# The last four heads' gate logits carried as eight more value columns through the attention

## The chip, the cores and the metric

The program runs on one core of a Trainium2 chip. Its time is the device time of one execution in microseconds; the median of three runs before the change is 687.24 us (686.25 to 689.11). Five instruction streams matter: PE (TensorE, with PEld for its weight loads), DVE (VectorE), ACT (ScalarE), POOL (GpSimd) and SP, which here only issues DMAs, one after the other.

## The reference

Four batches of eight heads, 768 positions, head dimension 64. Attention is masked: a query sees the keys whose six sign bits (of a product with `proj`) equal its own. The attention output is laid out as x, 3072 tokens by 512 (eight heads side by side), and goes into a mixture of eight experts in which every token gets one expert, greedily by its logit and with 384 tokens an expert.

```python
mask = q_bucket[:, :, :, None] == k_bucket[:, :, None, :]
scores = np.where(mask, scale * np.matmul(q, k.transpose(0, 1, 3, 2)), -1e9)
attn = np.exp(scores - np.max(scores, axis=-1, keepdims=True))
attn = attn / (np.sum(attn, axis=-1, keepdims=True) + 1e-09)
x = np.matmul(attn, v).transpose(0, 2, 1, 3).reshape(B * S, H * D)
logits = x @ w_gate                    # 3072 x 8
for idx in np.argsort(-logits.flatten()):
    tok, e = idx // E, idx % E         # first free place of the best logit
    if assigned[tok] >= 0 or counts[e] >= cap: continue
    assigned[tok] = e; counts[e] += 1
out[assigned == e] = np.maximum(x[assigned == e] @ w1[e], 0.0) @ w2[e]
```

The order of the logits decides, so they are kept near float32 by pairs of f16 or bf16 parts (a high part and the remainder).

## The kernel before, in words

The 32 heads are worked in eight groups G of four (two groups a batch; a group's tiles alternate between two buffers, u = G%2). Work advances in steps t, six to a head, and each step has two half slots 2t and 2t+1; `add(n, f, ...)` hangs a function on half slot n, and the numbers in the table `AP` say which. The instructions of each engine run in the order in which this loop writes them; there is no other scheduler.

For a head, in steps: `S_pass` (L240) computes a score tile for the row maxima, which DVE takes (L242, m), and `m_rows` (L248, L249) writes them into rows 96 to 127 of QA; these passes run about nine steps ahead. `ST` (L258, L259) computes the scores again, transposed and with the maximum taken off, into a `psT` bank (three of them), and ACT takes the exponential (L260, pt). `lo` (L263) makes the low part of pt, on POOL or, where the table `XL` names the step, on DVE. `AV` (L273 to L275), four steps later, multiplies by the values: 18 matmuls a step, of 65 or 64 columns (64 value columns and one of ones, which gives the row sum) into the only `psV` bank; after a head's sixth step six matmuls with WF (L279, L280) take off the masked keys' share. `norm` (L287 to L290) divides and writes x; after every second head the two are stored to `x_dram`. `xtr` (L300 to L302) transposes two heads' x with PE into XH and XL, and `logits` (L309 to L311) multiplies by the gate weights `wgs`.

The values reach VH (f16) by `cv` on ACT and VL (remainder) by `sv` on POOL. `sumv` and `sumw` (L204 to L214) sum them into WF.

On SP: `load` fetches q, k and v of the next group (768 KB each), `moves` copies the casts into QA, KA, QB, KB and the sign rows bt into rows 64 to 69, and `clear` (L191) writes zeros into rows 96 to 127 of the QA buffer that the next group uses, 192 KB. A score pass reads all 128 rows of QA, so it needs its group's clear, casts and signs.

After head 31 the routing starts: `best` (L496 to L520) and then phase 0 of `Moe.phase`, a long chain of short DVE and PE steps that ends in the row numbers of the first expert's tokens; those are gathered from `x_dram` (xg, L762), the weights wf are fetched (L770), and the two layers of eight experts follow on PE.

Of the kernel before, what the change touches and what calls it, by code (L numbers as in the profile page):

```python
# [45 lines left out]
def attention(tc, nc, ctx, qT, kT, vv, proj, wg, x_dram, L, jp, identf, B, late=None, after=None):  # L46
# [9 lines left out]
    LD={}  # L56
# [27 lines left out]
    wgs=cp.tile([128,4,2,8],F16,name="wgs")  # L84
# [107 lines left out]
    def cv(G,j): A.copy(VH[G%2][:,j,:,0:64],LD[G][2][:,j])  # L192
    def sv(G,j,e=None): (e or V).tensor_tensor(VL[G%2][:,j],LD[G][2][:,j],VH[G%2][:,j,:,0:64],op=ALU.subtract)
    SQ={}
    def sumv(G):
        u=G%2
        if G<2:
            A.copy(WF[u][96:128,:,64],wc[96:128,:].to_broadcast([32,4]))
        ps=psT.tile([128,512],F32,name="pst")
        n=0  # L200
        for c in range(6):
            for src in (VH[u],VL[u]):
                g=32*(n%4)
                T.matmul(ps[g:g+32,0:256].rearrange("p (j d) -> p j d",j=4),on,src[:,:,c,0:64],start=n<4,stop=n>7,skip_group_check=True,tile_position=(0,g)); n+=1  # L204
        SQ[G]=dp.tile([128,256],F32,name="sq",bufs=1)
        A.copy(SQ[G],ps[:,0:256])
    def sumw(G):
        u=G%2
        ps=psT.tile([128,512],F32,name="pst")
        T.matmul(ps[:,0:256],onf,SQ[G],start=True,stop=True)  # L210
        pv=ps[96:128,0:256].rearrange("p (j d) -> p j d",j=4)
        hi=dp.tile([128,4,64],F16,name="shi",bufs=1)
        A.copy(hi[96:128],pv)
        V.scalar_tensor_tensor(WF[u][96:128,:,0:64],hi[96:128],ml[96:128],pv,op0=ALU.mult,op1=ALU.add)  # L214
# [49 lines left out]
    AVt={}  # L264
    def AV(h,kc):
        G,j=divmod(h,4); u=G%2
        if kc==0: AVt[h]=psV.tile([128,512],F32,name="psv")
        av=AVt[h][:,0:390].rearrange("p (c d) -> p c d",c=6)
        p,l=PT[h,kc]
        ph=p.bitcast(BF)[:,1::2]  # L270
        for c in range(6):
            r=slice(c*128,c*128+128)
            T.matmul(av[:,c,:],ph[:,r],VH[u][:,j,kc,:],start=(kc==0 and c==0),stop=False,skip_group_check=True)  # L273
            T.matmul(av[:,c,0:64],ph[:,r],VL[u][:,j,kc,:],start=False,stop=False,skip_group_check=True)  # L274
            T.matmul(av[:,c,:],l[:,r],VH[u][:,j,kc,:],start=False,stop=False,skip_group_check=True)  # L275
        if kc==5:
            for c in range(6):

                if j==3: T.matmul(av[:,c,:],QA[u][96:128,j,c*128:c*128+128],WF[u][96:128,j,:],start=False,stop=(c==5),skip_group_check=True,tile_position=(96,0))  # L279
                else: T.matmul(av[:,c,:],QA[u][:,j,c*128:c*128+128],WF[u][:,j,:],start=False,stop=(c==5),skip_group_check=True)  # L280
    X={}
    def norm(h):
        b,hh=divmod(h,8)
        if hh==0: X[b]=dp.tile([128,6,512],F32,name="X")
        av=AVt[h][:,0:390].rearrange("p (c d) -> p c d",c=6)
        r=dp.tile([128,6],F32,name="r6")
        V.tensor_scalar(r,av[:,:,64],1e-9,None,op0=ALU.add)  # L287
# [9 lines left out]
    def xtr(b,d,hf):  # L297
# [17 lines left out]
    def add(n,f,*a): at.setdefault(n,[]).append((f,a))
# [16 lines left out]
    def slots(G): return AP['P1'] if G==1 else AP['P2'] if G==2 else AP['P3'] if G==3 else [48*(G-1)+x for x in AP['P4']]  # L332
# [15 lines left out]

    k=12; done={}; half={}; S_at={}
# [589 lines left out]


@with_exitstack
def tile_bucket_attention_moe(ctx, tc, qT, kT, vv, proj, wg, w1, w2, out):
    nc = tc.nc
    B = qT.shape[0] // 2
    drp = ctx.enter_context(tc.tile_pool(name="drp", bufs=1, space=DR))
    x_dram = drp.tile([768 * B, 512], F32, name="x_dram")
    M = Moe(tc, nc, ctx, 768 * B)
    late = M.consts()
    with ExitStack() as c1:
        c1.enter_context(tc.manual_schedule())  # L950
        attention(tc, nc, c1, qT, kT, vv, proj, wg, x_dram, M.Lm, M.jp, M.identf, B, late, M.early)
# [39 lines left out]
```

## Time and profile before

| what | value |
|---|---|
| median of three runs | 687.24 us |
| the profiled execution | 686.77 us |
| its span, first to last instruction | 685.0 us |
| outside the span | 1.8 us |
| busy share of the span | PE 97%, POOL 76%, DVE 73%, ACT 69% |
| chain that ended last, by engine | PE 78%, DVE 8%, DMA 6%, ACT 3% |

The attention fills the first 372 us, the routing's phase 0 the next 25, the experts the rest. In the attention every engine is busy most of the time, so a stretch has to be read by itself. A busy PE is read with care: a matmul's duration overlaps the next one's, so its price is the distance from one start to the next.

### The profile page before, as it was taken

How to read it: one execution, taken by the hardware profiler on the slowest of the kernel's cores; microseconds unless marked ns; L12 is line 12 of the kernel's file. 1: busy time of each engine (PE TensorE's matmuls, PEld its weight loads, DVE VectorE, ACT ScalarE, POOL GpSimd, SP SyncE). 2: the span in 40 equal slices, each digit the busy share in tenths (PEclk: the TensorE clock that was granted, in tenths of full speed). 3: DMA queues.
4: the chain of work that ended last, by engine and by line, in shares of the span. 5: the costliest groups of instructions: out<-in, count | busy, mean ns of one | idle time of the engine just before them, and what ended most of it. 6: DMA issues, size and time to landing. Idle time of an engine off the chain costs nothing.

```text
span 685.0 us, 19366 instructions
## 1 busy us (share of the span) xinstructions
PE 661.1 (97%) x7952; PEld 435.0 (64%) x7952; DVE 499.7 (73%) x1124; ACT 471.4 (69%) x887; POOL 518.8 (76%) x456
## 2 busy tenths in 40 slices
PE   8899999999999999999998799999999999999997
PEld 3567676777777777777766575555555555655553
DVE  6778889888877887878884688778777887734120
ACT  7879887888878878877764054765665656666760
POOL 7999997997998989988655156586776665779871
PEclk9999999999999999999999599999999999999999
DMA  8646755526546266340000161717271726271701
GB/s 228 196 117 209 176 167 137 136 82 164 166 110 164 72 150 175 93 105 25 25 24 28 57 237 27 282 47 292 62 277 55 284 83 242 77 277 67 272 32 46
DMA packets 40241, 93.59 MB, mean 137 GB/s; under 512 B 4581, under 2 KB 30553, under 8 KB 37849
## 3 DMA queue, kind: packets, MB, share of 16 engines
q1 hardware_dynamic: 33048, 46.21, 25.3%
q0 software_dynamic: 7104, 46.15, 19.0%
q8 instruction: 62, 1.02, 0.6%
q14 instruction: 27, 0.21, 0.1%
HBM read 59.53 MB, written 12.58 MB: 105 GB/s over the span
## 4 chain that ended last, share of the span: by engine, by line
PE 78%; DVE 8%; DMA 6%; ACT 3%; issue 2%; POOL 1%; SPq 1%; POOLq 0%; DVEq 0%; ACTq 0%
PE po L870 14%; PE px L858 13%; PE pst L258 9%; PE pst L259 8%; PE pss L240 8%; PE psv L273 5%; PE psv L275 5%; PE psv L274 4%; PE pst L300 2%; DMA wf<-in_w_dram,zwidx 2%; DVE m L242 1%; PE po L858 1%; PE pst L248 1%; DVE lo L263 1%; PE pss L142 1%
## 5 line engine op out<-in xcount | busy, mean ns | idle before, releaser
L263 POOL TENSOR_TENSOR lo<-pt 128x768 f16<-128x768 f32 x144 | 226.3, 1585 | 35.9 <-ACT pt L260 33.0
L260 ACT ACTIVATE pt<-pst 128x384 f32<-128x384 f32 x384 | 181.8, 491 | 59.0 <-PE pst L259 49.3
L242 DVE TENSOR_REDUCE m<-pss 128x1 f16<-128x770 f32 x192 | 181.2, 956 | 34.0 <-PE pss L240 32.7
L258 PE MATMUL pst<-qa,ka 128*128 128x384 f16 x384 | 125.1, 326 | 3.8 <-ACT qa L249 2.8
L259 PE MATMUL pst<-qb,kb 128*128 128x384 f16 x384 | 124.8, 325 | 0.0
L273 PE MATMUL psv<-vh,pt 128*128 128x65 f16 x1152 | 120.7, 194 | 0.5 <-DVE X L290 0.5
L275 PE MATMUL psv<-vh,lo 128*128 128x65 f16 x1152 | 120.8, 194 | 0.0
L274 PE MATMUL psv<-vl,pt 128*128 128x64 f16 x1152 | 120.8, 193 | 0.0
L273 PEld LDWEIGHTS <-pt 128*128 128x128 bf16 x1152 | 106.7, 98 | 8.7 <-issue 0.6
L274 PEld LDWEIGHTS <-pt 128*128 128x128 bf16 x1152 | 105.6, 99 | 8.8 <-issue 0.7
L275 PEld LDWEIGHTS <-lo 128*128 128x128 f16 x1152 | 105.8, 97 | 0.0
L797 POOL TENSOR_TENSOR wl<-wf,wh 128x512 f16<-128x512 f32 x74 | 83.7, 1157 | 21.5 <-ACT wf L788 20.9
L240 PE MATMUL pss<-ka,qa 128*128 128x385 f16 x384 | 94.0, 328 | 1.5 <-DMA ka<-bt 0.7
L779 ACT ACTIVATE wh<-wf 128x1024 f16<-128x1024 f32 x64 | 66.9, 1054 | 31.7 <-DMA wf<-in_w_dram,zwidx 31.7
L858 PEld LDWEIGHTS <-wh 128*128 128x128 f16 x480 | 45.3, 97 | 29.8 <-issue 0.8
L263 DVE TENSOR_TENSOR lo<-pt 128x768 f16<-128x768 f32 x48 | 61.1, 1273 | 1.9 <-ACT pt L260 1.8
L870 PEld LDWEIGHTS <-hh 128*128 128x128 f16 x384 | 35.8, 97 | 38.4 <-issue 0.4
L788 ACT ACTIVATE wf<-wf 128x1024 f32<-128x1024 f32 x55 | 57.9, 1059 | 0.9
L240 PEld LDWEIGHTS <-qa 128*128 128x128 f16 x384 | 37.0, 97 | 27.1 <-DMA qa<-bt 1.4
L875 ACT ACTIVATE o<-po 128x512 f32<-128x512 f32 x23 | 13.7, 597 | 56.8 <-PE po L870 51.4
L259 PEld LDWEIGHTS <-kb 128*128 128x128 f16 x384 | 37.4, 97 | 18.8 <-issue 6.8
L770 POOL DMA_INDIRECT wf<-in_w_dram,zwidx x22 | 25.6, 1163 | 30.6 <-DVE zSTb L661 12.0
(296 smaller groups left out, 1359.7 us busy)
## 6 DMA issues: line engine op xcount, KB each, us to landing
vp<-in_vv_dram SPq DMA_DIRECT2D x8, 768.0 KB
x_dram<-X SPq DMA_DIRECT2D x16, 384.0 KB
qp<-in_qT_dram SPq DMA_DIRECT2D x7, 768.0 KB
kp<-in_kT_dram SPq DMA_DIRECT2D x7, 768.0 KB
qa<-qh SPq DMA_DIRECT2D x14, 192.0 KB
qb<-qh SPq DMA_DIRECT2D x14, 192.0 KB
ka<-kh SPq DMA_DIRECT2D x14, 192.0 KB
kb<-kh SPq DMA_DIRECT2D x14, 192.0 KB
```

What stands on the lines that cost most here:

```text
L240: T.matmul(ps[:,hf,0:HK],QA[u][:,j,qc*128:qc*128+128],KA[u][:,j,hf*HK:hf*HK+HK],start=True,stop=True)
L242: V.tensor_reduce(M6[h][:,qc:qc+1],ps[:,:,0:HK],axis=AX.XY,op=ALU.max,negate=True)
L258: T.matmul(ps[:,0:384],KA[u][:,j,kr],QA[u][:,j,r],start=True,stop=False)
L259: T.matmul(ps[:,0:384],KB[u][:,j,kr],QB[u][:,j,r],start=False,stop=True)
L260: A.activation(PT[h,kc][0][:,r],ps[:,0:384],AF.Exp,scale=0.125)
L263: eng.tensor_tensor(l,p,p.bitcast(BF)[:,1::2],op=ALU.subtract)
L273: T.matmul(av[:,c,:],ph[:,r],VH[u][:,j,kc,:],start=(kc==0 and c==0),stop=False,skip_group_check=True)
L274: T.matmul(av[:,c,0:64],ph[:,r],VL[u][:,j,kc,:],start=False,stop=False,skip_group_check=True)
L275: T.matmul(av[:,c,:],l[:,r],VH[u][:,j,kc,:],start=False,stop=False,skip_group_check=True)
L797: for _ in range(n): s.nc.gpsimd.tensor_tensor(*s.pend.pop(0)[1],op=ALU.subtract)
L858: T.matmul(p[:,0:384],a[:,o:o+128],b[:,d],start=n==0,stop=n==11)
L870: T.matmul(p,a[:,f,c*128:c*128+128],b[:,f*512:f*512+512],start=n==0,stop=n==23)
```

## The change

For the last four heads (group 7) the value tiles get eight more columns in front: V times the gate weights of that head's 64 dimensions, times 16, as an f16 pair like V itself. They go through AV, WF and the division like value columns, so `norm` of heads 28 to 31 gets each head's part of the logits, 128x48, straight from the `psV` bank, scaled by the reciprocal of the row sum. Each part goes to a slot of its own in a tile pl; heads 24 to 27 give a fifth part by transposes and `logits` as before (now after head 27), and after head 31 one reduction over the five slots writes the logits. The transposes, splits and logits matmuls of heads 28 to 31 are gone. The last head's x is written by six ACT instructions in place of two on DVE.

V times gate is made in group 6: `vload` fetches V of group 7 transposed (`vT`, 768 KB) into the q buffer, four casts and two subtractions split it, `vw` multiplies (two times 18 matmuls of 16 columns), copies and casts, `vlow` makes the remainder. The gate weights are prepared by five small instructions.

The tiles of all groups are wider (73 and 72 columns); before group 7 the first eight columns are not read. `XL` moves four `lo` between POOL and DVE, `sumv` of group 7 moves from half slot 324 to 345, and `CL` moves every group's `clear` by two half slots.

```diff
- XL={2: [0, 5], ..., 20: [0, 5], 29: [0, 1, 5], 30: [2]},
+ XL={2: [0, 5], ..., 20: [0, 5], 27: [3, 5], 29: [0], 30: [2, 4], 31: [1, 3]},
- CL=9,
+ CL=11,
+ WV=345,
+ VW=[180, 288, 314, 317, 320, 323, 323, 327, 334, 334],
...
+    def low8(G): return 0 if G==NG-1 else 8
+    def vload():
+        LD[NG]=(dp.tile([128,2,S],F32,name="qp",bufs=1),); SY.dma_start(LD[NG][0],vT[NG-1])
+    def vw(p):
+        u=(NG-1)%2; js=slice(2*p,2*p+2); w=GW['w'][:,p].rearrange("p z h e -> p z (h e)"); ...
+        for c in range(6):
+            for a,z in ((h,0),(h,1),(l,0)): T.matmul(ps[:,c*16:c*16+16],a[:,r],w[:,z],...); n+=1
+        GW[p]=dp.tile([128,2,6,8],F32,name="sw")
+        A.copy(GW[p],ps[:,0:96].rearrange("p (c h e) -> p h c e",c=6,h=2))
+        A.copy(VH[u][:,js,:,0:8],GW[p])
...
-            T.matmul(av[:,c,:],ph[:,r],VH[u][:,j,kc,:],start=(kc==0 and c==0),...)
-            T.matmul(av[:,c,0:64],ph[:,r],VL[u][:,j,kc,:],...)
+            T.matmul(av[:,c,:],ph[:,r],VH[u][:,j,kc,o:],start=(kc==0 and c==0),...)
+            T.matmul(av[:,c,0:72-o],ph[:,r],VL[u][:,j,kc,o:],...)
...
-        for c0,c1 in ((0,3),(3,6)) if h==NH-1 else ((0,6),):
-            V.tensor_tensor(X[b][:,c0:c1,hh*64:hh*64+64],av[:,c0:c1,0:64],...)
+        def part():
+            if o: return
+            V.scalar_tensor_tensor(GW['p'][:,:,:,h%4],av[:,:,0:8],1.0/16,r[:,:,None].to_broadcast([128,6,8]),op0=ALU.mult,op1=ALU.mult)
+            if h==NH-1: V.reduce_sum(L[:,b*6:b*6+6],GW['p'],axis=AX.X)
+        if h==NH-1:
+            part()
+            for c in range(6): A.activation(X[b][:,c,hh*64:hh*64+64],av[:,c,8-o:72-o],AF.Copy,scale=r[:,c:c+1])
+        else:
+            V.tensor_tensor(X[b][:,:,hh*64:hh*64+64],av[:,:,8-o:72-o],...)
+            part()
...
-        if h==NH-1: n=2*(6*h+5+LAG)
+        if h<4*(NG-1):
+            for hf in range(2): add(m+AP['X'][1]*hf,xtr,b,d,hf)
+            if d==(1 if b==B-1 else 3): add(m+AP['X'][2],logits,b,range(d+1))
```

The order of instructions at the end of the attention: DVE from the last division to the first instruction of the routing. Before:

```order
L263 TENSOR_TENSOR lo<-pt 128x768 x2
L287 TENSOR_SCALAR r_8441<-psv 128x6
L288 RECIPROCAL r_8441<-r_8441 128x6
L290 TENSOR_TENSOR X<-psv,r_8441 128x3x64 x2
L302 TENSOR_TENSOR XT<-pst,XT 128x384 x2
L311 TENSOR_REDUCE Lm<-pss 128x48
L496 TENSOR_REDUCE zm<-Lm 128x6
```

After, where the line numbers are those of the changed kernel (r is the reciprocal of the row sum, pl the slots, Lm the logits, zm the routing's first tile):

```order
L287 TENSOR_TENSOR lo<-pt 128x768 x2
L313 TENSOR_SCALAR r_8485<-psv 128x6
L314 RECIPROCAL r_8485<-r_8485 128x6
L317 SCALAR_TENSOR_TENSOR pl<-psv,r_8485 128x48
L318 TENSOR_REDUCE Lm<-pl 128x48
L531 TENSOR_REDUCE zm<-Lm 128x6
```

Between the reciprocal and zm two DVE instructions stand in place of five, and none of the new ones waits for PE or ACT.

SP around the clear of group 2, the third group (qa_180 is its QA buffer, qa_184 the next group's; wrm holds zeros). Before:

```order
L61 DMA vp<-in_vv_dram 128x1536
L293 DMA x_dram<-X 128x6x128
L191 DMA qa_180<-wrm 32x8x384
L174 DMA qa_180<-qh 64x2x768 x2
L176 DMA qb_182<-qh 64x2x768 x2
L61 DMA qp<-in_qT_dram 128x1536
```

After, 18 rows further down the queue, behind the group's signs (bt) and the load of the next k (kp):

```order
L174 DMA qa_180<-bt 6x768
L174 DMA ka_181<-bt 6x768
L63 DMA kp<-in_kT_dram 128x1536
L193 DMA qa_180<-wrm 32x8x384
L327 DMA x_dram<-X 128x6x128
L63 DMA vp<-in_vv_dram 128x1536
```

The clear moved from ahead of all of the group's moves to behind them and behind a 768 KB load; in the other groups its place among SP's DMAs is the same as before.

## Rows read from the trace of the kernel before

**Rows 1.** Timeline, end of the attention: start us, us, engine, line, what.

```profile
372.44 0.62 DVE L290 TENSOR_TENSOR X<-psv,r 128x192 f32<-128x192 f32 x2
373.09 0.36 SPq L293 DMA_DIRECT2D x_dram<-X  x1
...
375.30 0.26 DVE L311 TENSOR_REDUCE Lm<-pss 128x48 f32<-128x96 f32 x1 [0.33 <-PE pss L310]
375.60 0.20 DVE L496 TENSOR_REDUCE zm<-Lm 128x6 f32<-128x48 f32 x1
...
400.62 0.34 DVE L496 TENSOR_REDUCE zm<-Lm 128x24 f32<-128x192 f32 x1
```

**Rows 2.** Chain that ended last: start us, us, what.

```profile
337.07 0.33 PE pst L300 x3
...
393.96 3.85 DMA xg<-x_dram,zidx
```

**Rows 3.** Timeline of PE: value matmuls, logits matmuls and 128-column matmuls.

```profile
360.45 0.19 PE L273 MATMUL psv<-vh,pt 128*128 128x65 f16 x1
...
360.99 0.33 PE L258 MATMUL pst<-qa,ka 128*128 128x384 f16 x1
...
361.32 0.30 PE L309 MATMUL pss<-wgs,XT 128*128 128x16 f16 x6
...
362.22 0.32 PE L258 MATMUL pst<-qa,ka 128*128 128x384 f16 x1
...
403.35 0.39 PE L843 MATMUL px<-xl,wh 128*128 128x128 f16 x4
403.57 0.39 PE L843 MATMUL px<-xh,wh 128*128 128x128 f16 x4
```

**Rows 4.** Groups by line and shape, 327 to 372 us: busy us, mean ns | idle before.

```profile
L273 PE MATMUL psv<-vh,pt 128*128 128x65 f16 x178 | 18.4, 194 | 0.5 <-DVE X L290 0.5
...
L274 PEld LDWEIGHTS <-pt 128*128 128x128 bf16 x177 | 16.2, 99 | 1.6 <-issue 0.7
```

**Rows 5.** Windows: length, busy us of PE, PEld, DVE, ACT, POOL; PEclk, DMA, GB/s.

```profile
300.00:318.00 18.00, 18.00 (x288) 13.56 (x286) 15.30 (x23) 13.54 (x29) 16.20 (x14) 1.00 0.23 64
318.00:327.00 9.00, 9.00 (x148) 6.52 (x144) 7.25 (x15) 6.45 (x14) 5.13 (x4) 1.00 0.01 2
...
335.00:345.00 10.00, 9.44 (x133) 6.93 (x132) 9.53 (x13) 7.66 (x16) 3.36 (x3) 1.00 0.14 43
345.00:357.00 12.00, 11.51 (x199) 8.77 (x196) 10.32 (x16) 7.49 (x16) 8.04 (x5) 1.00 0.01 2
357.00:372.00 15.00, 14.62 (x304) 11.57 (x302) 5.39 (x9) 9.13 (x21) 10.10 (x7) 1.00 0.09 28
```

**Rows 6.** One line each: casts on ACT, subtractions on POOL; ns least/median/most.

```profile
L128 ACT CAST qh<-qp x28: 500/512/515, 31.1 to 281.8; 128x384 f16<-128x384 f32 x28
L130 POOL TENSOR_TENSOR ql<-qp,qh x15: 1636/1644/1658, 14.2 to 282.4; 128x768 f16<-128x768 f32 x15
```

**Rows 7.** Timeline of SP's queue around group 2's clear.

```profile
73.46 0.70 SPq L191 DMA_DIRECT2D qa<-wrm  x1
74.27 0.63 SPq L174 DMA_DIRECT2D qa<-qh  x1
...
92.06 0.44 SPq L61 DMA_DIRECT2D kp<-in_kT_dram  x1
```

**Rows 8.** Windows around head 8's first score pass, columns as in Rows 5.

```profile
92.00:93.00 1.00, 1.00 (x39) 1.00 (x36) 1.00 (x2) 0.49 (x1) 1.00 (x1) 1.00 0.05 14
93.00:94.00 1.00, 1.00 (x17) 0.73 (x14) 0.94 (x3) 0.30 (x1) 1.00 (x1) 1.00 0.73 258
94.00:95.00 1.00, 1.00 (x9) 0.50 (x7) 0.99 (x2) 0.95 (x3) 1.00 (x2) 1.00 0.96 387
95.00:96.00 1.00, 1.00 (x14) 0.73 (x14) 1.00 (x2) 1.00 (x3) 1.00 (x2) 1.00 0.80 272
```

**Rows 9.** Timeline of PE: head 8's first score pass.

```profile
93.44 0.49 PE L240 MATMUL pss<-ka,qa 128*128 128x385 f16 x2
```

More of the change, by code (lines that the diff above doesn't have):

```diff
@@ L45, with attention @@
 EMPTY=60000.0
-def attention(tc, nc, ctx, qT, kT, vv, proj, wg, x_dram, L, jp, identf, B, late=None, after=None):
+def attention(tc, nc, ctx, qT, kT, vv, vT, proj, wg, x_dram, L, jp, identf, B, late=None, after=None):
     S=768; NG=2*B; NH=8*B; LAG=4
@@ L191, in clear, with cv, sv, gate_blocks @@
         SY.dma_start(QA[G%2][96:128].rearrange("p j (z q) -> p (j z) q",z=2),wrm[0:32,None,0:384].to_broadcast([32,8,384]))
-    def cv(G,j): A.copy(VH[G%2][:,j,:,0:64],LD[G][2][:,j])
-    def sv(G,j,e=None): (e or V).tensor_tensor(VL[G%2][:,j],LD[G][2][:,j],VH[G%2][:,j,:,0:64],op=ALU.subtract)
+    def cv(G,j): A.copy(VH[G%2][:,j,:,8:72],LD[G][2][:,j])
+    def sv(G,j,e=None): (e or V).tensor_tensor(VL[G%2][:,j,:,8:72],LD[G][2][:,j],VH[G%2][:,j,:,8:72],op=ALU.subtract)
+    def low8(G): return 0 if G==NG-1 else 8
+    GW={}
+    def gate_blocks(n):
+        if n==0: GW['f']=dp.tile([128,2,2,8],F32,name="wb",bufs=1); GW['w']=dp.tile([128,2,2,2,8],F16,name="wz",bufs=1); G_.memset(GW['f'],0.0)
+        elif n<3: A.mul(GW['f'][64*n-64:64*n,:,n-1],wgr[64*n-64:64*n,2:4],16.0)
+        elif n==3: A.copy(GW['w'][:,:,0],GW['f'])
+        else: G_.tensor_tensor(GW['w'][:,:,1],GW['f'],GW['w'][:,:,0],op=ALU.subtract)
+    def vload():
+        LD[NG]=(dp.tile([128,2,S],F32,name="qp",bufs=1),); SY.dma_start(LD[NG][0],vT[NG-1])
+        for k,n in (('h',"qh"),('l',"ql")): TMP[NG,k]=[dp.tile([128,2,S],F16,name=n,bufs=1)]
+    def vw(p):
+        u=(NG-1)%2; js=slice(2*p,2*p+2); w=GW['w'][:,p].rearrange("p z h e -> p z (h e)"); h,l=(TMP[NG,k][0][:,p] for k in 'hl')
+        ps=psT.tile([128,512],F32,name="pst"); n=0
+        for c in range(6):
+            r=slice(c*128,c*128+128)
+            for a,z in ((h,0),(h,1),(l,0)): T.matmul(ps[:,c*16:c*16+16],a[:,r],w[:,z],start=n==0,stop=n==17,skip_group_check=True); n+=1
+        GW[p]=dp.tile([128,2,6,8],F32,name="sw")
+        A.copy(GW[p],ps[:,0:96].rearrange("p (c h e) -> p h c e",c=6,h=2))
+        A.copy(VH[u][:,js,:,0:8],GW[p])
+    def vlow(p):
+        u=(NG-1)%2; js=slice(2*p,2*p+2)
+        G_.tensor_tensor(VL[u][:,js,:,0:8],GW[p],VH[u][:,js,:,0:8],op=ALU.subtract)
     SQ={}
     def sumv(G):
-        u=G%2
+        u=G%2; w=72-low8(G)
         if G<2:
-            A.copy(WF[u][96:128,:,64],wc[96:128,:].to_broadcast([32,4]))
+            A.copy(WF[u][96:128,:,72],wc[96:128,:].to_broadcast([32,4]))
         ps=psT.tile([128,512],F32,name="pst")
@@ L203, in sumv @@
                 g=32*(n%4)
[L204 to L206 removed]
+                T.matmul(ps[g:g+32,0:4*w].rearrange("p (j d) -> p j d",j=4),on,src[:,:,c,72-w:72],start=n<4,stop=n>7,skip_group_check=True,tile_position=(0,g)); n+=1
+        SQ[G]=dp.tile([128,288],F32,name="sq",bufs=1)
+        A.copy(SQ[G][:,0:4*w],ps[:,0:4*w])
     def sumw(G):
[L208 removed]
+        u=G%2; w=72-low8(G)
         ps=psT.tile([128,512],F32,name="pst")
[L210 to L214, printed above, removed]
+        T.matmul(ps[:,0:4*w],onf,SQ[G][:,0:4*w],start=True,stop=True)
+        pv=ps[96:128,0:4*w].rearrange("p (j d) -> p j d",j=4)
+        hi=dp.tile([128,4,72],F16,name="shi",bufs=1)
+        A.copy(hi[96:128,:,0:w],pv)
+        V.scalar_tensor_tensor(WF[u][96:128,:,72-w:72],hi[96:128,:,0:w],ml[96:128],pv,op0=ALU.mult,op1=ALU.add)
     def top(j):
@@ L302, in xtr @@
         V.tensor_tensor(XL[:,d,r],p,XH[:,d,r],op=ALU.subtract)
-    LP=[]
     def logits(b,ds):
-        if ds[0]==0: LP.append(psS.tile([128,2,512],F32,name="pss")[:,0] if b==B-1 else psT.tile([128,512],F32,name="pst"))
-        p=LP[-1][:,0:96].rearrange("p (c z e) -> p c z e",c=6,z=2)
+        p=psT.tile([128,512],F32,name="pst")[:,0:96].rearrange("p (c z e) -> p c z e",c=6,z=2)
         for d in ds:
             for c in range(6): T.matmul(p[:,c],XH[:,d,c],wgs[:,d],start=(d==0 and c==0),stop=False,skip_group_check=True)
-            for c in range(6): T.matmul(p[:,c,0],XL[:,d,c],wgs[:,d,0],start=False,stop=(d==3 and c==5),skip_group_check=True)
-        if ds[-1]==3: V.reduce_sum(L[:,b*6:b*6+6],p.rearrange("p c z e -> p c e z"),axis=AX.X)
+            for c in range(6): T.matmul(p[:,c,0],XL[:,d,c],wgs[:,d,0],start=False,stop=(d==ds[-1] and c==5),skip_group_check=True)
+        if b==B-1: GW['p']=dp.tile([128,6,8,5],F32,name="pl",bufs=1)
+        V.reduce_sum(GW['p'][:,:,:,4] if b==B-1 else L[:,b*6:b*6+6],p.rearrange("p c z e -> p c e z"),axis=AX.X)
     at={}
@@ L344, in attention @@
         for j in range(4): add(p[15]+st*j,cv,G,j); add(p[15]+st*j+sg,sv,G,j,G_)
-        if G==NG-1: add(p[18],sumv,G)
-        add((slots(G+1)[12] if G<NG-1 else p[18])+AP['SW'],sumw,G)
+        if G==NG-1: add(AP['WV'],sumv,G)
+        add((slots(G+1)[12] if G<NG-1 else AP['WV'])+AP['SW'],sumw,G)
         if G>1: add(48*(G-1)+AP['CL'],clear,G)
@@ L356, in attention @@
     for h in range(1,NH,2):
-        b,d=h//8,h%8//2; n=2*(6*h+5+LAG)+AP['X'][0]
-        if h==NH-1: n=2*(6*h+5+LAG)
-        for hf in range(2): add(n+AP['X'][1]*hf,xtr,b,d,hf)
-        if d==3: add(n+(4 if b==B-1 else AP['X'][2]),logits,b,[3] if b==B-1 else range(4))
-        elif d==2 and b==B-1: add(n+4,logits,b,range(3))
+        b,d=h//8,h%8//2; n=2*(6*h+5+LAG); m=n+AP['X'][0]
+        if h<4*(NG-1):
+            for hf in range(2): add(m+AP['X'][1]*hf,xtr,b,d,hf)
+            if d==(1 if b==B-1 else 3): add(m+AP['X'][2],logits,b,range(d+1))
         if after and d==3:
             for i,f in enumerate(after(b,lambda: psT.tile([128,512],F32,name="pst"),lambda: psV.tile([128,512],F32,name="psv"))):
-                add(n+5 if b==B-1 else max(n+8,AP['EA'][b][0])+AP['EA'][b][1]*i,f)
+                add(n if b==B-1 else max(m+8,AP['EA'][b][0])+AP['EA'][b][1]*i,f)
+    W=AP['VW']; add(W[1],vload)
+    for n in range(5): add(W[0]+12*n,gate_blocks,n)
+    for n in range(4): add(W[2+n],cast,NG,0,n//2,n%2)
+    for p in range(2): add(W[6+p],sub,NG,0,p); add(W[8+p],vw,p); add(W[8+p]+1,vlow,p)
     for n,f in enumerate(late or ()): add(AP['L0'][0]+AP['L0'][1]*n,f)
@@ L941, in tile_bucket_attention_moe @@
 @with_exitstack
-def tile_bucket_attention_moe(ctx, tc, qT, kT, vv, proj, wg, w1, w2, out):
+def tile_bucket_attention_moe(ctx, tc, qT, kT, vv, vT, proj, wg, w1, w2, out):
     nc = tc.nc
@@ L950, in tile_bucket_attention_moe @@
         c1.enter_context(tc.manual_schedule())
-        attention(tc, nc, c1, qT, kT, vv, proj, wg, x_dram, M.Lm, M.jp, M.identf, B, late, M.early)
+        attention(tc, nc, c1, qT, kT, vv, vT, proj, wg, x_dram, M.Lm, M.jp, M.identf, B, late, M.early)
     with ExitStack() as c2:
```

29 lines of the change are left out of this document (16 added, 13 removed).

## The prediction

> **What bounds the kernel now.** I read the chain of waits first: in the attention it is PE almost alone, at the attention's end it leaves PE for a stretch of short waits, and later it passes through the gather of x [rows 2]. Then the windows: from 300 to 327 us PE is busy in all of the time, so whatever PE gets there is paid in full unless something else gives way; from 335 to 372 us it is idle for 0.56, 0.49 and 0.38 us, 1.43 us together, because DVE (9.53 of 10 us, then 10.32 of 12) or ACT is late [rows 5]. Third, the timeline of the tail: from the end of head 31's reciprocal to the routing's first instruction 3.16 us go by (372.44 to 375.60), a relay DVE, PE, ACT, DVE, PE, DVE in which nobody works ahead [rows 1]. Last, SP's queue and the windows beside it, because the change of one number moves a DMA there.
>
> So a piece of work counts in one of three ways: on PE before 372 us nearly at its price, in the relay at its full latency, and on the other engines only where PE waits for them.
>
> **The tail.** After the reciprocal, DVE now computes the last part of the logits and one reduction, and is then at the routing. The part reads 48 elements a partition from the `psV` bank. The nearest rows: 0.20 us for 48 elements, 0.26 us for 96 from PSUM, 0.34 us for 192 [rows 1]. I take 0.26 us for the part and, for the reduction of 240 elements, 0.40 us (from 48 to 192 elements the price rises by 0.14 us, so by 0.05 more for another 48), and 0.03 us between dependent instructions, as between 375.30 plus 0.26 and 375.60. The new stretch is 0.72 us against 3.16, a gain of 2.45 us. Bounds: the cheapest rows give 0.6 us, and 0.35 and 0.6 us for the two give 1.0; the gain lies between 2.15 and 2.55 us.
>
> What could be late instead? The counting matmuls that stood behind the logits on PE run earlier and were never waited for. The last x is written by six ACT instructions, about 0.25 us each, so until some 374 us, and its store to `x_dram` leaves 0.9 us later than the 373.09 of now [rows 1]; the gather that needs it starts at 393.96 [rows 2], so 17 us cover it. The same six hold the `psV` bank, which PE's warm-up matmuls want again some 2.7 us after the reciprocal; 1.2 us of cover. Everything behind the routing's first instruction hangs on it in one chain, so the 2.45 us should reach the end.
>
> **PE before the tail.** The value matmuls of four heads get eight columns more: 4 x 6 x 18 of them and 24 with WF, 456. Eighteen with 65 or 64 columns take 0.54 us from start to start (360.45 to 360.99), 30 ns each; four with 128 columns take 0.22 us (403.35 to 403.57), 55 ns; 36 with 16 or 8 columns take 0.90 us (361.32 to 362.22), 25 ns each [rows 3]. Between 64 and 128 columns a column costs 0.39 ns, so eight cost 3.2 ns and 456 matmuls 1.45 us. Between 12 and 65 columns the slope is only 0.1 ns; if that held further, it would be 0.35 us. Pro rata to 30 ns it would be 1.7. I take 1.45, because above 64 columns the matmuls of this kernel follow the first slope.
>
> Each of these matmuls has a weight load of its own, busy for 99 ns, and yet the matmuls start 30 ns apart [rows 3, 4]: the loads run ahead and beside one another. [...]
>
> `vw` adds 36 matmuls of 16 columns, 0.90 us at 25 ns. The wider `sumv` and `sumw` add about 0.1 us (an eighth more columns). Heads 24 to 27 now need their own logits matmuls, 24 at 25 ns, 0.60 us; the 36 that stood before head 31's end go, 0.90 us [rows 3]; two groups of three transposes go, 0.33 us each [rows 2]. Sum: 1.45 + 0.90 + 0.10 + 0.60 - 0.90 - 0.66 = 1.5 us more on PE before the tail.
>
> Part of it fills idle time. The 1.43 us of 335 to 372 us are waits for engines that are late; a PE that has more to do reaches them later. One is 0.5 us, for a `norm` on DVE [rows 4], and `XL` takes two `lo` of head 29 off DVE there; two transposed groups leave ACT and DVE too. I take 0.8 us back; bounds 0 and 1.43.
>
> **The other engines.** Four casts at 0.51 us and four small copies are about 3 us more on ACT, two subtractions at 1.64 us 3.3 us more on POOL [rows 6], in steps that fall between 309 and 327 us. ACT is busy 13.54 of 18 and 6.45 of 9 us, POOL 5.13 of the last 9 [rows 5]; there is room, but a cast ahead of an exponential delays a `psT` bank by up to half a microsecond. I put 0.3 us on PE's account; bounds 0 and 0.8. `vload` stands on SP ahead of group 7's moves and has to wait for that group's last q subtraction, so the moves start some 2 us later; they are needed 15 us later. Each `norm` of heads 28 to 30 holds `psV` for 0.25 us more; PE still has score matmuls in between.
>
> **The clear.** With `CL` at 11, group 2's clear falls behind `moves` in the same half slot, so on SP it stands behind the signs and behind the load of the next k. In the old order it was issued at 73.46 us, 20 us ahead of need; k's load went out at 92.06 [rows 7]. Now it goes out right behind that load. Head 8's first score pass reads the rows that it writes and began on PE at 93.44 without idle time before it [rows 9]. How late the zeros are: the load moves 768 KB, and the windows show 258 KB in the microsecond from 93, 387 in the next and the rest by about 95.5; the zeros, 192 KB at these rates, need 0.5 to 0.8 us more: 96.0 to 96.3 [rows 8]. The queue is earlier by at least the 0.81 us that the clear took at its old place (73.46 to 74.27) [rows 7], so 95.2 to 95.5, and PE stands still for 1.9 us. Bounds: 0, if the zeros pass the load or the pass is reached later; 2.9, if the queue gains nothing. I take 1.9, and 0.5 of it comes back, since POOL, busy in all of 92 to 96 us, catches up meanwhile [rows 8]: 1.4 us.
>
> [...]
>
> **Sum.** -2.45 + 1.5 - 0.8 + 0.3 + 1.4 = 0.0 us. Against the profiled execution's 686.77 us that is 686.8; the median of the runs lies 0.47 us higher, so I forecast 687.2 us. Half a per cent, 3.4 us, is what a measurement of this kernel can tell from no change.
>
> **Rivals.**
> - *The clear costs nothing* (the pass is reached late enough, or the wait is given back before group 3): 686.77 - 2.45 + 1.0 = 685.3, 685.8 by the median; with all 1.43 us of idle time filled as well, 685.2. For it: the attention's engines trade slack with one another. Against: PE has no idle time in 92 to 96 us. Chance 0.27.
> - *Slower: PE stands at head 8's first score pass for 2.9 us, gets nothing of it back and finds no idle time to fill later.* -2.45 + 1.5 + 0.3 + 2.9 = 2.25: 689.0, 689.5 by the median. It decides from a wait of about 0.7 us on, where it outweighs what the tail then leaves after PE's own additions (2.45 - 1.5 - 0.3). For it: the queue's rows. Against: the queue had to wait for earlier landings too. Chance 0.18.
> - *The tail's gain is not passed on*, so that the change does not do what it says: the routing waits for ACT's hold of the bank or for x. 686.8 + 2.45 = 689.2, 689.7 by the median. Against: the covers above. Chance 0.07.
> - *The eight columns are free*: 685.3, 685.8 by the median. Against: the 30 and 55 ns. Chance 0.05.
> - My forecast: 0.43; its own range 686 to 688.5.
>
> The range runs from all bounds that help, -2.55 + 1.5 - 1.1 (columns at 0.35 us) - 1.43 = -3.6, which is 683.2 and 683.7 by the median, to all that hurt, -2.15 + 1.5 + 0.8 + 2.9 = 3.1, which is 689.8 and 690.3, with a little over for the bank's hold. Faster by over 0.5% (below 683.8) needs free zeros, nearly free columns and filled gaps together: 0.13. Slower by over 0.5% (above 690.7) needs the slow rival and a tail that is not passed on: 0.10. Within: 0.77.
>
> **What would show it.** In the new timeline: from the reciprocal's end to zm 0.7 us; value matmuls of heads 28 to 31 33 ns apart; an idle time of PE of about 2 us before head 8's first L264 with a DMA into qa as its end; less idle time of PE from 335 us to the end of head 31. I am wrong if that wait is under 0.5 us (then the time is near 685.5) or if the tail's stretch is over 1.2 us.

## The result, and the profile after

The changed kernel takes 691.17 us (median of six executions, 690.22 to 693.15); the kernel before, beside it on the same chip, took 686.67 (686.25 to 689.11). The ratio is 1.0065, with a 95% interval of 1.0044 to 1.0086: slower by 0.65%, above the 690.7 us to which I had given a chance of 0.10. I had forecast 687.2 us and a range to 690.3 with a little over.

The profiled execution of after has a span of 691.4 us (before 685.0); it is the slowest of the six (693.15), so the spans differ by 6.4 us where the medians differ by 4.5. Both programs pass the same marks, so the spans can be cut there: the first score pass of heads 4, 8, 9 and 28 on PE, the norm of head 31 on DVE, the end. This table, worked out from the starts in the traces of all runs that follow, carries most of what I have to say (us):

| run | to head 4 | 4 to 8 | 8 to 9 | 9 to 28 | 28 to norm 31 | to the end |
|---|---|---|---|---|---|---|
| before | 49.57 | 43.87 | 10.51 | 209.42 | 58.65 | 312.98 |
| after | 49.99 | 48.48 | 11.97 | 209.42 | 60.66 | 310.85 |
| e1 after, clears at 9 | 48.95 | 43.79 | 10.51 | 209.42 | 60.66 | 312.80 |
| e2 before, clears at 11 | 48.73 | 47.39 | 11.99 | 209.50 | 58.65 | 314.13 |
| e3 clear ahead of the load | 49.77 | 44.28 | 10.44 | 209.41 | 60.66 | 310.91 |
| e4 PE kept busy | 48.73 | 49.09 | 10.43 | 209.44 | 60.69 | 311.41 |
| e5 clear from ACT | 48.72 | 48.55 | 13.12 | 209.41 | 60.68 | 311.31 |
| e6 clear between halves | 49.09 | 45.82 | 10.43 | 209.44 | 60.68 | 309.98 |
| e7 old lo table | 50.13 | 43.81 | 10.51 | 209.41 | 60.63 | 312.01 |
| e8 columns unread | 49.96 | 43.81 | 10.51 | 209.44 | 59.42 | 310.25 |
| e9 old lo, 29 and 30 | 48.93 | 43.88 | 10.51 | 209.41 | 60.34 | 312.64 |
| e10 lo 29: 3, 5 | 49.70 | 43.88 | 10.51 | 209.44 | 60.63 | 310.78 |
| e11 lo 29: 5 | 50.12 | 43.88 | 10.51 | 209.42 | 60.64 | 310.22 |

The middle columns repeat to 0.1 us wherever nothing was changed; the first varies by 1.4 us from one execution to the next, the last by 2.8 among the runs with the new tail. The loss sits in two columns: 4.6 us from head 4 to 8, 1.5 from head 8 to 9; the 2.0 us more up to norm 31 and the 2.1 us less behind it cancel. Nothing of it comes back from head 9 to 28.

The first is the wait that I had named, more than twice as long. SP's queue in after, the answer to [rows 7] (start, length of the issue):

```profile
92.40 0.38 SPq L63 DMA_DIRECT2D kp<-in_kT_dram  x1
92.89 0.73 SPq L193 DMA_DIRECT2D qa<-wrm  x1
```

The clear stands right behind the load of k. PE's timeline, the answer to [rows 9], with the idle time ahead of an instruction in brackets:

```profile
93.63 0.32 PE L283 MATMUL pst<-qb,kb 128*128 128x384 f16 x1
98.47 0.49 PE L264 MATMUL pss<-ka,qa 128*128 128x385 f16 x2 [4.51 <-DMA kp<-in_kT_dram]
98.80 0.33 PE L272 MATMUL pst<-ident,m 128*128 128x128 f16 x3
...
99.51 0.53 PE L282 MATMUL pst<-qa,ka 128*128 128x384 f16 x1
99.83 0.53 PE L283 MATMUL pst<-qb,kb 128*128 128x384 f16 x1
```

The view puts the 4.51 us down to the load, but it was the clear: in the trace the last of the load's 16 completion signals comes at 97.49 us, the last of the clear's at 98.38, 0.09 us ahead of the pass. e3 and e6 show the same by moving it. From 99.51 us the same matmuls start 0.32 us apart instead of 0.16. The windows (columns as in [rows 5]), which answer to [rows 8], say why: the granted clock, the third number from the right, falls from 1.00 to 0.50 about 0.6 us behind the stand, as I call the time in which PE stands still ahead of a pass, and stays there for 3.4 us.

```profile
93.00:94.00 1.00, 0.95 (x23) 0.57 (x19) 1.00 (x3) 0.00 (x0) 1.00 (x1) 1.00 0.98 114
94.00:95.00 1.00, 0.00 (x0) 0.00 (x0) 0.85 (x4) 0.49 (x1) 1.00 (x2) 1.00 0.61 172
95.00:96.00 1.00, 0.00 (x0) 0.00 (x0) 0.00 (x0) 0.00 (x0) 1.00 (x1) 1.00 1.01 350
...
99.00:100.00 1.00, 1.00 (x7) 0.52 (x5) 0.96 (x1) 0.81 (x2) 0.00 (x0) 0.52 0.97 393
100.00:101.00 1.00, 1.00 (x5) 0.59 (x3) 0.00 (x0) 0.83 (x2) 0.52 (x1) 0.50 0.33 127
101.00:102.00 1.00, 1.00 (x5) 0.66 (x5) 0.96 (x1) 0.33 (x1) 0.95 (x1) 0.50 0.00 0
102.00:103.00 1.00, 1.00 (x21) 0.86 (x20) 0.56 (x1) 0.65 (x2) 0.12 (x1) 0.77 0.00 0
```

The tail did what it was meant to. The answer to [rows 1]:

```profile
380.72 0.19 DVE L314 RECIPROCAL r<-r 128x6 f32<-128x6 f32 x1
380.94 0.25 DVE L317 SCALAR_TENSOR_TENSOR pl<-psv,r 128x48 f32<-128x48 f32 x1
381.22 0.40 DVE L318 TENSOR_REDUCE Lm<-pl 128x48 f32<-128x240 f32 x1
381.28 1.33 ACT L321 ACTIVATE X<-psv,r 128x64 f32<-128x64 f32 x6 [3.55 <-DVE pl L317]
381.66 0.20 DVE L531 TENSOR_REDUCE zm<-Lm 128x6 f32<-128x48 f32 x1
...
382.64 0.36 SPq L327 DMA_DIRECT2D x_dram<-X  x1
```

From the part's start to the routing 0.72 us go by, as forecast, where 3.16 us went by.

And the value matmuls: 18 of 73 or 72 columns, then the next score matmul, the answer to [rows 3]. 0.59 us against 0.54, 33 ns each.

```profile
367.91 0.20 PE L299 MATMUL psv<-vh,pt 128*128 128x73 f16 x1
...
368.50 0.33 PE L282 MATMUL pst<-qa,ka 128*128 128x384 f16 x1
```

### The profile page after: what moved, and what is told of

Same layout as the page of the kernel before. It is cut to its first block, busy times and chain, and to the rows that moved or that the text cites. A ratio compares the mean times of both kernels' runs of the same rounds, so it can differ in the third digit from the quotient of the medians.

```text
span 691.4 us, 19387 instructions
## 1 busy us (share of the span) xinstructions
PE 663.6 (96%) x7952; PEld 436.6 (63%) x7952; DVE 502.0 (73%) x1124; ACT 474.7 (69%) x900; POOL 523.8 (76%) x461
## 4 chain that ended last, share of the span: by engine, by line
PE 77%; DMA 7%; DVE 7%; ACT 3%; issue 2%; SPq 2%; POOL 1%; POOLq 0%; ACTq 0%; DVEq 0%
PE po L905 15%; PE px L893 12%; PE pst L282 8%; PE pst L283 8%; PE pss L264 7%; PE psv L299 5%; PE psv L301 4%; PE psv L300 4%; DMA ka<-kh 2%; DMA wf<-in_w_dram,zwidx 2%; PE pst L334 1%; PE pss L144 1%; PE po L893 1%; PE pst L272 1%; DVE m L266 1%
## 5 line engine op out<-in xcount | busy, mean ns | idle before, releaser
L300 PE MATMUL psv<-vl,pt 128*128 128x64 f16 (+1 forms) x1152 | 122.2, 193 | 0.0
L301 PE MATMUL psv<-vh,lo 128*128 128x65 f16 (+1 forms) x1152 | 122.2, 194 | 0.0
L299 PE MATMUL psv<-vh,pt 128*128 128x65 f16 (+1 forms) x1152 | 122.2, 195 | 0.0
L299 PEld LDWEIGHTS <-pt 128*128 128x128 bf16 x1152 | 107.5, 98 | 9.1 <-issue 1.0
L301 PEld LDWEIGHTS <-lo 128*128 128x128 f16 x1152 | 106.7, 97 | 0.0
L287 DVE TENSOR_TENSOR lo<-pt 128x768 f16<-128x768 f32 x49 | 62.9, 1285 | 4.8 <-ACT pt L284 4.5
L273 ACT ACTIVATE qa<-pst,mbi,msc 32x384 f16<-32x384 f32 x64 | 42.4, 662 | 10.4 <-PE pst L272 7.2
```

The source lines that it names most:

```text
L299: T.matmul(av[:,c,:],ph[:,r],VH[u][:,j,kc,o:],start=(kc==0 and c==0),stop=False,skip_group_check=True)
L300: T.matmul(av[:,c,0:72-o],ph[:,r],VL[u][:,j,kc,o:],start=False,stop=False,skip_group_check=True)
L301: T.matmul(av[:,c,:],l[:,r],VH[u][:,j,kc,o:],start=False,stop=False,skip_group_check=True)
```

## The experiments

Ratios are to the kernel before, run on the same chip beside each.

**e1: only the clear undone.** In the changed kernel:

```diff
- CL=11,
+ CL=9,
```

> The changed kernel with the clears at 9 as before the change; all else of the change stays. My theory, that the clear of group 2 is what made it slower: the first score pass of head 8 begins at 93.8 us with no idle time ahead of it, the granted clock stays at 1.00 there, the profile is 6 us shorter and the median 685 to 686.5 us, so no slower than before the change. Rival, that the slow part is the work of group 7 (eight more columns, the value products, the moved subtractions) and the stand at head 8 is given back later: 690 us or more.

Measured: 686.55 us, ratio 0.9989 (0.9974 to 1.0004). The median is just above the range that I had named. PE reaches head 8's pass without idle time ahead of it; the load of k goes out at 92.06 us, as before the change:

```profile
92.74 0.49 PE L264 MATMUL pss<-ka,qa 128*128 128x385 f16 x2
```

The whole loss was the clear, and of the clears that of group 2: from head 9 to norm 31 this run and after take the same time. The rest of the change moves the time by -1.8 to +0.3 us; my other terms had said -1.45, and the table says -0.4 (2.0 longer from head 28 to norm 31, 2.4 shorter in the tail).

**e2: only the clear, in the kernel before** (`CL=9` to `CL=11`).

> The kernel before with the clears at 11 alone. My theory: PE stands 3 to 5 us ahead of the first score pass of head 8, its clock then falls to half for 2 to 3 us, and the time is 690.5 to 693 us (4 to 6 more). Rival, that only together with the rest of the change the clear comes late (the queue of SP is later by 0.3 us there): under 688.5 us.

Measured: 690.58 us, ratio 1.0047 (1.0028 to 1.0066). That lies in the range that I had named, but by the ratio it is only 3.2 us more than the kernel before beside it (1.9 to 4.5), at the low end of my 4 to 6 or under it. The wait and the half clock are there without any of the rest:

```profile
96.12 0.49 PE L240 MATMUL pss<-ka,qa 128*128 128x385 f16 x2 [3.38 <-DMA kp<-in_kT_dram]
```

```profile
97.00:98.00 1.00, 1.00 (x5) 0.48 (x4) 0.61 (x1) 0.97 (x2) 0.00 (x0) 0.50 1.01 399
```

Here SP's queue did gain what I had counted on: the load went out at 90.09, 1.13 us earlier than before if both are counted from head 4's pass, and the wait is 1.1 us shorter than in after, where it went out only 0.08 us earlier by the same count. This count scatters from one execution to the next; the section on the prediction's steps says by how much.

**e3: the clear ahead of the load.** Same half slot, one place forward on SP:

```diff
-        elif G==2: ...; low(); signs(); nxt(1)
+        elif G==2: ...; low(); signs(); clear(2); nxt(1)
...
-        if G>1: add(48*(G-1)+AP['CL'],clear,G)
+        if G>2: add(48*(G-1)+AP['CL'],clear,G)
```

> The changed kernel with the clear of group 2 in the same half slot as in it, behind the signs, but ahead of the load of the next k on SP's queue instead of behind it: it goes out near 92.0 us, some 0.8 us earlier. Theory A, that the zeros wait for the bytes of the load ahead of them: they land near 94.5 us, PE stands for under 1.5 us, its clock stays up, and the time is within 1 us of the kernel with the clears at 9. Theory B, that the transfers share the engines and that the late issue is what costs: they land near 96.5 us or later, PE stands for 2.5 us or more, and the time is 689 us or more.

Measured: 687.51 us, ratio 1.0009 (0.9989 to 1.0029). SP's queue and PE:

```profile
91.06 0.72 SPq L193 DMA_DIRECT2D qa<-wrm  x1
91.82 0.60 SPq L63 DMA_DIRECT2D kp<-in_kT_dram  x1
```

```profile
94.05 0.50 PE L264 MATMUL pss<-ka,qa 128*128 128x385 f16 x2 [0.32 <-DMA qa<-wrm]
```

PE's wait is 4.2 us shorter than in after, and the 1.5 us of clock are gone. Not all of it is the one place on the queue: counted from head 4's pass, SP was 1.1 us earlier in this execution than in after. Of the rest 0.5 us is the load's own issue, 2.0 us the zeros' way behind its bytes, and 0.6 us the way from their last packet to PE's start. The packets show the order: in this window all are under 2 KB, as the zeros' are (768 bytes; the load's rows have 6144).

```profile
DMA packets 223, 0.17 MB, mean 145 GB/s; under 512 B 0, under 2 KB 223, under 8 KB 223
```

That is 92.2 to 93.38 us. In after, the same view of 93.3 to 96.0 us has only the load's:

```profile
DMA packets 103, 0.63 MB, mean 234 GB/s; under 512 B 0, under 2 KB 0, under 8 KB 103
```

Theory A stands: with the load ahead the zeros' first packet moved 2.5 us behind the end of their issue (93.62 to 96.07), and here 0.65 us behind it.

**e4: PE kept busy while it waits.** In the changed kernel, ahead of the pass:

```diff
+        for _ in range(32 if (h,qc)==(8,0) else 0): T.matmul(ps[:,0,0:384],wrm[:,0:128],wrm[:,0:384],start=True,stop=True)
```

> The changed kernel with 32 matmuls of 384 columns, which compute nothing that is used, on PE just ahead of the first score pass of head 8 (5.1 us at full clock). My theory, that PE's stand costs a second time because its clock falls to half behind it: the granted clock stays at 1.00 from 99 to 103 us, and the profile is 1 to 2 us shorter than the changed kernel's 693.15 (the median 689 to 690.5). Rival, that the slower stretch behind the stand only follows the late inputs of the other engines: no gain, 691 to 692 us.

Measured: 691.81 us, ratio 1.0074 (1.0046 to 1.0101). PE, and its windows:

```profile
92.62 5.36 PE L263 MATMUL pss<-wrm 128*128 128x384 f16 x32
97.82 0.49 PE L265 MATMUL pss<-ka,qa 128*128 128x385 f16 x2
```

```profile
93.00:98.00 5.00, 5.00 (x33) 2.99 (x32) 0.73 (x2) 0.37 (x1) 3.35 (x3) 1.00 1.03 341
98.00:103.00 5.00, 5.00 (x65) 3.68 (x64) 3.90 (x5) 3.98 (x9) 2.89 (x2) 1.00 0.12 52
```

The clock stays at 1.00 and head 8 to 9 takes 10.43 us again, not 11.97: the second loss is the clock's. The median shows no gain; the 32 matmuls took 5.2 us where the stand had been 4.5, so that by head 9 only 0.9 us were won, which the interval can't tell. For the time the rival's 691 to 692 us came true, but not for its reason.

**e5: the clear from another queue.** ACT issues it, behind its exponentials from 90.04 us on:

```diff
-        SY.dma_start(QA[G%2][96:128]...
+        (A if G==2 else SY).dma_start(QA[G%2][96:128]...
...
+        if G>1: add(77 if G==2 else 48*(G-1)+AP['CL'],clear,G)
```

> The changed kernel with the clear of group 2 alone issued by ACT, behind its third exponential of 91.3 to 92.9 us, so on another queue than SP's load of the next k and later than that load. Theory A, that the zeros came late because they stood behind the load's bytes on one queue: they land 2 to 2.5 us after their issue, near 95 us, and PE stands for 1 to 2 us ahead of head 8's first score pass. Theory B, that all transfers share the 16 engines and these were full: PE stands for 3 us or more, as in the changed kernel (4.5 us).

Measured: 694.29 us (two executions), ratio 1.0090 (1.0055 to 1.0125). The two issues and the wait:

```profile
91.13 0.72 ACTq L193 DMA_DIRECT2D qa<-wrm  x1
```

```profile
91.31 0.39 SPq L63 DMA_DIRECT2D kp<-in_kT_dram  x1
```

```profile
97.26 0.82 PE L264 MATMUL pss<-ka,qa 128*128 128x385 f16 x2 [4.58 <-DMA qa<-wrm]
```

Theory A as I had put it, that one common queue is the reason, falls: from a queue of its own the clear is as late. It took 0.72 us to issue, until 91.85, and the load only 0.39, until 91.70. The packets (queue: count, MB, share of the 16 engines' time): from 92.2 to 95.1 us there are the load's alone, on its queue q1, 111 of its 128; the ACT queue q10 moves in the window behind it, 95.1 to 96.6.

```profile
q1 hardware_dynamic: 111, 0.68, 89.3%
```

```profile
q1 hardware_dynamic: 326, 0.25, 62.4%
q10 hardware_dynamic: 272, 0.20, 43.7%
```

The wait is the one that B named, but even sharing is not what these rows show: nothing of the zeros moved until 95.18 us, and only the load's last packets, which end at 95.85, overlap with them. Why the load's bytes went first is not shown: which engine moved what the trace does not tell.

**e6: the clear between two halves of the load.** The clear's own slot is taken out as in e3.

```diff
-        elif G==2: ...; signs(); nxt(1)
+        elif G==2: ...; signs(); SY.dma_start(LD[3][1][:,0],kT[3][:,0]); clear(2); SY.dma_start(LD[3][1][:,1],kT[3][:,1])
```

> The changed kernel with the load of k ahead of group 2's clear cut into two halves of 384 KB, and the clear between them on SP. Theory A, that the DMA engines take the work in the order in which it was issued, from whatever queue (in the run with the clear from ACT the zeros' packets of 768 B moved only behind the load's of 6144 B, and those were issued first): the zeros follow 384 KB, their packets move 1.2 to 2 us earlier against the first half's issue than they did behind the whole load, and PE stands for 1.5 to 3 us. Theory B, that the engines share their time between all that is outstanding, so that the zeros end with the load whatever its place: PE stands for 4 us or more.

Measured: 688.27 us, ratio 1.0029 (1.0013 to 1.0045), between e3 and after, as A has it.

```profile
94.90 0.49 PE L264 MATMUL pss<-ka,qa 128*128 128x385 f16 x2 [1.77 <-DVE X L323]
```

The releaser named is wrong (that DVE instruction feeds no score pass); the clear's zeros moved from 92.47 to 93.96 us and the last of its completion signals came at 94.81. Their last packet was 3.7 us behind the first half's issue, where it was 5.1 us behind the whole load's in after. Head 8 to 9 takes 10.43 us: behind a stand of 1.77 us the clock did not fall, behind 3.38 and 4.51 it did.

**e7, e9, e10, e11: which `lo` of the last heads DVE computes**, all with the clears at 9. The change's `XL` moves seven `lo`, not four: five to DVE, and two of head 29 to POOL. Sets for head 29 and 30 on DVE: after `[0]`, `[2, 4]`; e7 the old table wholly (27, 31 and these); e9 `[0, 1, 5]`, `[2]`; e10 `[3, 5]`, `[2]`; e11 `[5]`, `[2]`. The question is the stretch from head 28 to norm 31, 2.0 us longer than before.

> The changed kernel with the clears at 9 and with the old table for the subtractions of lo (heads 27, 29, 30 and 31). My theory: DVE's lo of head 29 takes 0.95 to 1.3 us again in place of the 2.24 us that it took at 345.26 beside POOL's two, PE's wait of 1.12 us for the row maximum at 348 us goes, and head 8's pass to head 31's norm takes 279.5 us or less (280.6 with the new table). Rival, that the new table is needed because POOL has two subtractions more (3.3 us) in this group: PE waits as long for a lo elsewhere, no shorter.

> The changed kernel with the clears at 9 and the old table for heads 29 and 30 alone, the new one kept for heads 27 and 31. My theory: as with the old table wholly, the wait of 1.12 us at 348 us goes, 279.5 us or less from head 8's pass to head 31's norm, and the time is 685 to 686.5 us. Rival: DVE has one lo more by head 31 and becomes late there, 280.5 us or more.

> The changed kernel with the clears at 9, and of head 29's subtractions of lo those of 3 and 5 on DVE (0 alone in the changed kernel, 0, 1 and 5 before), of head 30's that of 2. What was left with the old table there was PE's wait of 0.66 us at 349.5 us for the bank that head 28's norm reads, behind a lo of 1.25 us on DVE. My theory: with that lo on POOL, which is idle from 338 to 347 us, the wait goes, 279.9 us or less from head 8's pass to head 31's norm (280.27 with the old table for heads 29 and 30), and the time is 0.5 to 1.5 us under the kernel before. Rival: two of POOL's subtractions in a row (3 us) are late for head 29's value products, 280.5 us or more.

> As the run before, with only 5 of head 29's subtractions of lo on DVE. My theory: as there or 0.2 us better, since DVE has one less by head 29's norm. Rival: POOL, with five of six, is late for the value products by 0.5 us or more.

Measured: 60.63, 60.34, 60.63 and 60.64 us against 60.66; ratios 0.9994 (0.9982 to 1.0007), 0.9992 (0.9977 to 1.0007), 0.9984 (0.9974 to 0.9994), 0.9979 (0.9970 to 0.9988). My theories for the stretch fall: e9 gains 0.3, the others nothing. I was right on the cause of the one wait and wrong on what its end is worth. e10's time lies where I had put it, 0.9 us under the kernel beside it, but the stretch that was to bring this is no shorter: the number came out without its reason. In e1, on DVE and on POOL:

```profile
342.20 0.94 DVE L287 TENSOR_TENSOR lo<-pt 128x768 f16<-128x768 f32 x1
...
345.26 2.24 DVE L287 TENSOR_TENSOR lo<-pt 128x768 f16<-128x768 f32 x1
```

```profile
345.22 3.60 POOL L287 TENSOR_TENSOR lo<-pt 128x768 f16<-128x768 f32 x2 [5.92 <-ACT pt L284]
```

A `lo` takes DVE 0.94 us while POOL is idle and 2.24 when POOL began one 0.04 us earlier. After has the same pair, 0.04 us apart at 352.4 us and 2.24 us on DVE; there POOL's first `lo` took 1.47 us. By an estimate from these rows the two one behind the other would take 1.47 and 0.94, 2.4 us, so most of DVE's 2.24 could be a wait for POOL's; that was not tried by itself. In e7 and e9 that `lo` takes 0.96 us and PE's 0.96 us wait for the row maximum goes; a wait of 0.50 us for the bank that head 28's norm holds comes in its place. In e11 another pair meets (POOL's `lo` began at 343.39 us, 0.08 us ahead of DVE's):

```profile
343.47 2.20 DVE L287 TENSOR_TENSOR lo<-pt 128x768 f16<-128x768 f32 x1
```

```profile
PE pst L282 <- DVE wf L238: 0.8, 1, 0.8
```

e11 has the lowest ratio here, 0.2% under the kernel before; that it owes this to the table is not shown, since its stretch is as long as e1's and the two intervals overlap.

**e8: the eight columns not read**, with the clears at 9:

```diff
-        o=low8(h//4); return ...
+        o=8; return ...
```

> The changed kernel with the clears at 9, and the value products of the last four heads without the eight gate columns (65 and 64 columns again; the last part of the logits then reads value columns, which leaves the gate's share of these heads out). Theory A, 3.2 ns for eight columns (my forecast): PE reaches head 31's norm 1.4 us sooner after head 28's first score pass than with them (60.66 us). Theory B, columns almost free: under 0.5 us sooner.

Measured (one execution): 59.42 us against 60.66, 1.24 us less. By the starts of the value matmuls alone the columns cost 1.47 us (L299 to L301, L305, L306: 22.76 us with them, 21.29 without); a longer wait for the row maximum (1.2 us in place of 1.0) took 0.2 back. Theory A holds.

## Why the prediction was wrong, by its steps

**The clear: the step that failed.** I had named place, cause and order, and they were right: PE waited for zeros that stood behind the load. That they would move behind its bytes was my estimate, which no row of before shows; after and e3 show it, with 2.5 and 0.65 us from the end of their issue to their first packet. The price was not right. I had put it at 1.9 us less 0.5 given back. In after it is 4.5 us, nothing given back, and 1.5 us of half clock, 6.0 in all. The sum of the wait, by the trace of after: the load went out at 92.40, where I had 92.06 less 0.81 (+1.15); from there to the last packet of zeros it took 5.1 us, until 97.51, where the rates of before gave 4.1 (+1.0); from that packet to PE's start it took 0.96, which I had left out; PE came to the pass 0.5 later (-0.5). 1.9 + 2.6 = 4.5.

- *The load's way.* From its issue to the last zero 5.1 us went by in e2 as well, and 6.0 in e4. The zeros' own part was right: their last packet ended 0.78 us behind the load's, where I had 0.5 to 0.8. The load's part was not. I had read its end as 95.5, 3.4 us behind its issue. By its packets it ended at 95.86 in before (3.8 us behind the issue), 4.0 us behind it in e1 and 4.3 us in after. In after it was slow from its start: 286 KB in the two windows from 93 us against 645 before [rows 8]. e1, without a clear behind its load, was slow in the first of these too (154 KB, where before moved 258 and after 114). What causes it stays open.
- *From the last packet to PE.* Left out of the sum: 0.96 us in after, 0.92 in e2.
- *The queue's gain.* It is there in the mean, but one trace can't show it. Counted from head 4's pass, the first DMA behind the signs went out after 41.1 to 42.4 us in the five profiles with group 2's clear behind the signs on SP (mean 41.65), and after 42.2 to 43.9 in the seven with the clears at 9 (mean 42.78); e5, with the clear on ACT, has 42.6. Between the two means lie 1.1 us, where I had 0.81 at least. Before and after, at 42.49 and 42.41, happen to lie near each other in that scatter, so the gain is missing in the sum above.
- *The give-back.* I had argued that POOL catches up meanwhile. Heads 9 to 28 take 209.4 to 209.5 us in all thirteen profiles, so nothing is ever caught up there: what PE has lost by head 9 stays lost.
- *The clock.* Not in my sum at all. Its price by both levels: e4 and after, 11.97 less 10.43, 1.5 us.

These are single executions, and after's is the slowest of its six. By the ratios the clear costs 5.2 us in the changed kernel (after less e1) and 3.2 us in the old one (e2), each within some 1.5 us, where the traces say 6.0 and 4.9.

The slower rival, with nothing given back and no idle time filled, was the right one, and with its 2.9 us still too cheap: it too had neither the clock nor the way from the last packet to PE. For a time above 690.7 us I had wanted a tail that is not passed on as well; that was not needed.

**The tail: right.** -2.45 forecast; 0.72 us in place of 3.16, -2.44. It seems to be passed on: the ten profiles with it (without e8, which routes otherwise) take 311.3 us from norm 31 to the end in the mean, the two without it 313.6. Single executions spread by as much (2.8 us), so this is shown in the mean alone, and roughly.

**PE before the tail: right.** +1.5 forecast. In brackets what I had: the columns 1.47 us (1.45), the 36 starts of `vw` 0.91 (0.90), the logits 0.61 added and 0.91 gone (0.60 and 0.90). The six transposes that went freed 0.86 us (0.66): I had read their price from the chain and not from start to start. `sumv` and `sumw` cost 0.19 (0.10), and the other matmuls 0.2 more (nothing), so that the sum comes out this near is in part luck. PE's busy time from head 28 to norm 31:

```profile
319.85:380.52 60.67, 58.82 (x985) 44.81 (x983) 47.92 (x70) 40.45 (x87) 41.88 (x30) 1.00 0.07 22
```

58.82 us, and 57.22 of 58.65 in the same stretch of before: 1.6 more. Columns are not free, so the rival that made them so falls.

**Idle time filled: wrong.** -0.8 forecast, and +0.3 for other engines; measured +0.4 together, 1.85 us idle where 1.43 was. PE's waits in before, without one of 0.2 us, and then in after:

```profile
PE pst L258 <- ACT qa L249: 0.5, 1, 0.5
PE psv L273 <- DVE X L290: 0.5, 1, 0.5
```

```profile
PE pst L272 <- DVE m L266: 1.0, 1, 1.0
PE pst L282 <- ACT qa L273: 0.7, 2, 0.5
```

The wait for the row bias on ACT is of the same size before and after: 0.50 us near 336 us in before and e1 alike, and 0.21 and 0.20 near 358 and 360. It is a relay that PE itself starts (score pass, maximum on DVE, transposes on PE, row bias on ACT, score matmul); more work on PE ahead of it shifts the relay with PE and fills nothing. That such relays are not filled is read from these rows and was not tried by itself. The wait for head 28's `norm`, which I had counted on, did go, as `XL` took `lo` off DVE there. But in its place came the first wait of after, 0.96 us for the row maximum, from DVE and POOL meeting; with the old table for heads 29 and 30 (e7, e9) it goes and the 0.5 us are back.

With the terms as measured the sum for the profiled execution is -2.44 + 1.6 + 0.4 + 6.0 = +5.6 us. It was late by another 0.42 at head 4 already and lost 0.3 behind the tail, which gives the 6.4 by which the spans differ. The medians differ by 4.5.

## What to carry to other kernels

When a small transfer that someone waits for moves on a queue, price the bytes that now stand ahead of it, from the issue to the waiter's start and not to the last packet (here 768 KB ahead of 192 KB: 6.1 us from the load's issue to PE's start), and add what the clock loses if TensorE stands for long (here it fell behind 3.38 us and not behind 1.77, and cost 1.5 us). Here another queue did not help (e5: a stand of 4.58 us, the load's bytes first); one place earlier did (e3: 0.32 us). And a queue's start that scatters by a microsecond (here 41.1 to 42.4 us) can't be read from one trace. Before idle time is counted as fillable, look whether the late engine's work starts at the engine that idles.

## What the runs showed of the hardware that was not expected

- TensorE's granted clock stayed at 1.00 behind a stand of 1.77 us (e6). With stands of 3.38 (e2), 4.51 (after) and 4.58 us (e5) it fell to 0.50: about 0.5 and 0.6 us behind the end of the first two, and in e5 some 1.0 us ahead of its end (0.77 in the window of 96.0 to 96.5 us, 0.50 from 96.5 on). It stayed low for 3.4 us in e2 and in after, and in e5 until 103 us at least, where head 8 to 9 took 13.12 us.
- A 768 KB load was taken by the 16 engines ahead of 192 KB from another issuer's queue whose issue began 0.18 us earlier and ended 0.15 us later (e5): the first zeros moved at 95.18 us, with 111 of the load's 128 packets begun by 95.1.
- DVE's and POOL's `lo`, begun 0.04 us apart, took 2.24 us on DVE instead of 0.94 (e1).
